# Loading token tiles in two groups ahead of the second weights, and regrouping the first products of a 2:4-pruned matrix product

## The chip, the cores and the metric

The kernel runs on one core of one Trainium2 chip. The metric is the device time in microseconds (us) of one execution, the median of several runs.

## What is computed

The weights `w` (1024 x 1024, bf16) are pruned 2 of 4: of each four neighbouring rows of a column, those two stay whose magnitude is the largest. The tokens `x` (16 x 512 = 8192 tokens of 1024 values) are multiplied with the pruned weights, and a bias is added.

```python
B, S, D = 16, 512, 1024
G = D // 4
wg = w.reshape(G, 4, D)
mag = jnp.abs(wg)
order = jnp.argsort(mag, 1)
thr = jnp.take_along_axis(mag, order[:, 2:3, :], 1)   # the second largest of four
mask = (mag >= thr).astype(w.dtype)
wp = (wg * mask).reshape(D, D)
return jnp.einsum("bsd,df->bsf", x, wp) + b
```

## The kernel before

The 8192 tokens are 64 tiles of 128. The 1024 rows of `w` are two groups g of 512; the columns of group 0 come in four pieces of 256 (pieces 0 to 3), those of group 1 in two of 512 (pieces 4 and 5). On the chip, the four members of a pruning group lie in one partition, as m = 0 to 3 of `w_sb`, so that VectorE can compare them: `abs` (magnitude), `hi` and `lo` (larger and smaller of two pairs), `t1`, `t2` and `thr` (the threshold), `mask`, and `mult` (the pruned weights, written to `wp`). These are the steps of the class `Piece` (from line 153).

There are two ways to multiply. In the natural way the pruned weights are moved by DMA from `wp` to `wp_nat` (`spread`, line 149), with the rows of `w` in the partitions, and the tokens come transposed by DMA (`xlead`, `xlow`, `xb`); this is `nat` (line 241), and nearly all of the work runs so. At the start, however, `wp_nat` isn't there yet. So the first seven tiles (0 to 6) are treated with group 0 in another way: they are loaded as they are (`load_x`, line 105), TensorE transposes each in four matmuls (`transpose`, line 194, token T), ScalarE copies the result from PSUM to SBUF (`copy_xt`, line 202, token C), and TensorE multiplies it straight with the pieces of `wp` as VectorE finishes them (`mm_piece`, line 215, token M; `M5.0t` is tile 5, piece 0, part t). A part is a choice of the members: u, v, s, t are m = 0, 1, 2, 3, x is the first two and y the last two. ScalarE copies finished sums of these products from PSUM to SBUF (`stage`, tokens S and U), where they wait for the other half of the product. Then follow the natural products: E and A open tiles 7 to 11, 24 half tiles are closed, and six batches of 8 tiles and one of 4 end the work.

The order on each engine is written out by hand. `order` (lines 267 to 289) holds one list of tokens for TensorE, VectorE, ScalarE and the SyncE queue; each engine executes its list in order. Ahead of the lists stand the loads, in the order of lines 122 to 134, split between the SyncE queue and, where "act" is given, ScalarE's queue:

```python
    load_w(0, 0, 256, 0, 2)
    load_w(0, 0, 256, 2, 4, "act")
    load_x(5, 6, "act")
    load_x(SOLO, SOLO + 1, "act")        # tile 6
    ...
    load_x(3, 5)
    load_w(0, 256, 512)                  # the second weights
    load_x(2, 3)
    load_x(0, 2)
```

The transposes write to a pool of two PSUM banks (`psum_t`); tile 4 alone takes one of the six banks of `psum_o`, where the products' sums lie too. A transpose therefore waits for the copy of the transpose two before it, except T4a. Before the lists TensorE runs 20 filler matmuls on constants, and the token F4 runs four more after T6a.

In SyncE's list W0.0 and W0.1 are the spreads of group 0's two column halves, W1.0p and W1.1 those of group 1 (W1.0q is on ScalarE's queue), Z the last weights and the bias, X1, Y1 and Y0 transposed loads.

Of the kernel before, what the change touches and what calls it, by code (L numbers as in the profile page):

```python
# [10 lines left out]
def kernel(  # L11
# [8 lines left out]
    P = 128  # L20
    bf16 = mybir.dt.bfloat16
    fp32 = mybir.dt.float32
# [10 lines left out]
    FH = 512  # L33
# [26 lines left out]
    psum_t = ctx.enter_context(tc.tile_pool(name="psum_t", bufs=2, space=bass.MemoryType.PSUM))  # L60
    psum_o = ctx.enter_context(tc.tile_pool(name="psum_o", bufs=6, space=bass.MemoryType.PSUM))
# [10 lines left out]
    def pe(i):  # L72
        return seq("pe", i)
# [4 lines left out]
    def act(i):  # L78
        return seq("act", i)

    def sp(i):
        return seq("sp", i)
# [10 lines left out]
    def tokens(dram, t):  # L93
        a, b_ = next(s for s in GROUPS if s[0] <= t < s[1])
        return dram[a * P:b_ * P].rearrange("(p t) k -> p t k", p=P), t - a
    bias_sb = const.tile([P, Dout], bf16)

    def issue(eng, out_, in_):
        q = nc.sync if eng == "sp" else nc.scalar
        return seq(eng, q.dma_start(out_, in_))  # L100

    def load_w(g, c0, c1, ma=0, mb=4, eng="sp"):
        issue(eng, w_sb[:, g, ma:mb, c0:c1], wv[:, g, ma:mb, c0:c1])

    def load_x(ta, tb, eng="sp"):
        xs = const.tile([P, tb - ta, HK], bf16, name=f"x_{ta}")
        xv, n = tokens(xf, ta)
        issue(eng, xs[:], xv[:, n:n + tb - ta, :HK])
        for t in range(ta, tb):
            x_sb[t] = xs[:, t - ta, :]  # L110
# [10 lines left out]

    load_w(0, 0, 256, 0, 2)
    load_w(0, 0, 256, 2, 4, "act")
    load_x(5, 6, "act")
    load_x(SOLO, SOLO + 1, "act")
    act(nc.scalar.activation(spark[:], nc.const_aps.tensor(1.0, [P, 1], bf16), Act.Abs))
    load_x(3, 5)
    load_w(0, 256, 512)
    load_x(2, 3)
    load_x(0, 2)  # L130
    load_w(0, 512, 768)
    load_w(0, 768, 1024)
    load_w(1, 0, 512)
# [7 lines left out]
    def filler(n, rep=1):  # L141
        for _ in range(n):
            pe(nc.tensor.matmul(warm_ps[:, :rep * P], lhsT=nc.const_aps.tensor(1.0, [P, P], bf16),  # L143
                                rhs=nc.const_aps.tensor(1.0, [P, rep * P], bf16), start=True, stop=True))
# [45 lines left out]
                self.tt(wp[:, self.g, ms, self.c0:self.c1], self.w[:, ms, :], self.mag[:, ms, :], Alu.mult)  # L190

    xpk = {}

    def transpose(t):
        xg = x_sb[t].rearrange("p (q m) -> p m q", m=4)
        bank = psum_o.tile([P, FH], fp32, name="ps") if t == 4 else psum_t.tile([P, FH], fp32, name="tp")
        tp = bank[:].bitcast(bf16)[:, :FH].rearrange("p (m q) -> p m q", m=4)
        for m in range(4):
            pe(nc.tensor.transpose(tp[:, m, :], xg[:, m, :], ident[:]))  # L199
        xpk[t] = tp  # L200
# [59 lines left out]
    def stage(key):  # L260
        solo = key[1] == "h"
        q, h, at = (pair_of[key[0]], key[2], int(key[0] != SOLO)) if solo else (key[0], key[1] // 2, key[1] % 2)
        if (q, h) not in staged:
# [2 lines left out]

    order = {
# [7 lines left out]
        ),  # L275
        "dve": (
# [4 lines left out]
        ),  # L281
        "act": (
            "C5a C3a C4a C6a C2a C0a C1a S3b0 S2b0 abs3 S0b0 U6h0 S3b1 S0b1 S2b1 S3b2 S0b2 S2b2 S2b3 S0b3 U6h1 "
            "S3b3 U7h0 W1.0q U7h1"
        ),
        "sp": (
            "W0.0 Z W0.1 X1 W1.0p Y1 Y0 W1.1"
# [1 line left out]
    }  # L289
    written = {"X0"}  # L290
    p = {}
    halves = {0: tuple("uvst"), 1: ('x', 'y'), 2: ('u', 'v', 'y'), 3: ('x', 'y')}

    by_rows = {0}

    def all_of(tok, i):
        return [tok + x for x in halves.get(i, ("",))]

    def split_tok(tok):
        k = tok[-1] if tok[-1] in "xyabuvst" else ""  # L300
        return (tok[:-1] if k else tok), k

    transposed = []

    def needs(eng, tok):
        base, k = split_tok(tok)
        if tok[0] == "C":
            return ["T" + tok[1:]]
        if tok[0] == "T":
            return ["C" + transposed[-2]] if tok != "T4a" and len(transposed) > 1 else []  # L310
        if tok[0] == "F":
            return []
        if tok[0] == "W":
            g, h = map(int, tok[1:4].split("."))
            return [n for i, pc in enumerate(pieces) if pc[0] == g and pc[1] // FH == h for n in all_of(f"mult{i}", i)]
        if tok[0] in "XYZ":
            return []
        if tok[0] == "A":
            return ["X0", f"W0.{tok.split('h')[1]}"] + ([f"U{NPK}h{tok[-1]}"] if tok[1] == "3" else [])
        if tok[0] == "E":  # L320
            return ["X0", f"W0.{tok[1]}"]
        if tok[0] == "U":
            t, h = map(int, tok[1:].split("h"))
            if t == NPK:
                return [f"E{h}"]
            return [f"M{t}.{x}" for i, pc in enumerate(pieces) if pc[0] == 0 and pc[1] // FH == h for x in all_of(str(i), i)]
        if base[0] == "M":
            t, i = base[1:].split(".")
            return [f"C{t}a", f"mult{i}{k}"]
        if tok[0] == "S":  # L330
            q, n = map(int, tok[1:].split("b"))
            return [f"M{t}.{x}" for i, pc in enumerate(pieces) if pc[0] == 0 and pc[1] // CW == n
                    for t in pairs[q] for x in all_of(str(i), i)]
        i, step = base[-1], base[:-1]
        before = {"abs": [], "hi": ["abs"], "lo": ["abs"], "t1": ["hi"], "t2": ["lo"],
                  "thr": ["t1", "t2"], "mask": ["thr", "hi", "lo"], "mult": ["mask"]}[step]
        out_ = []
        for b_ in before:
            if b_ in ("abs", "hi", "lo") and int(i) in by_rows:
                out_ += [b_ + i + k] if step in ("hi", "lo") else [b_ + i + s for s in "ab"]  # L340
            else:
                out_.append(b_ + i + (k if b_ == "mask" else ""))
        return out_

    def emit(eng, tok):
        base, k = split_tok(tok)
        if tok[0] == "T":
            transpose(int(tok[1:-1]))
            if tok != "T4a":
                transposed.append(tok[1:])  # L350
        elif tok[0] == "F":
            filler(int(tok[1:]))
        elif tok[0] == "W":
            g, h = map(int, tok[1:4].split("."))
            spread(g, h * FH, (h + 1) * FH, {"": range(4), "p": range(2), "q": range(2, 4)}[tok[4:]], eng)
        elif tok[0] == "Z":
            load_w(1, 512, 1024)
            sp(nc.sync.dma_start(bias_sb[:], b.partition_broadcast(P)))
        elif tok[0] == "X":
            xnat.update(load_lead(int(tok[1:])))  # L360
        elif tok[0] == "Y":
            xnat.update(load_low(int(tok[1:])))
        elif tok[0] == "E":
            open_solo(int(tok[1:]))
        elif tok[0] == "U":
            t, h = map(int, tok[1:].split("h"))
            stage((t, "h", h))
        elif tok[0] == "A":
            open_nat(*map(int, tok[1:].split("h")))
        elif tok[0] == "C":  # L370
            copy_xt(int(tok[1:-1]))
        elif tok[0] == "M":
            mm_piece(*map(int, base[1:].split(".")), part[k])
        elif tok[0] == "S":
            stage(tuple(map(int, tok[1:].split("b"))))
        else:
            i = int(base[-1])
            if i not in p:
                p[i] = Piece(i)
            if eng == "act":  # L380
                p[i].abs_act()
            else:
                p[i].do(base[:-1], part[k], half.get(k, slice(0, 2)))
# [82 lines left out]
    for bi, (tb, nb) in enumerate(batches):  # L466
        if bi:
            load_batch(bi + 1)
        for j in range(nb):
            t = tb + j  # L470
            xt = xnat[t]
            o = outp.tile([P, Dout], bf16, name="o")
            if t == NT - 1:
                for n, (c0, c1) in enumerate(((0, FH), (FH, FH + CW), (FH + CW, Dout - P), (Dout - P, Dout))):
                    ps = psum_o.tile([P, FH], fp32, name="ps")
# [44 lines left out]
```

## Time and profile before

| | |
|---|---|
| time, median of 3 runs | 233.68 us (233.33 to 234.12) |
| span of the profiled execution, first to last instruction | 232.0 us |
| time beside the span, median less span | 1.7 us |
| TensorE busy | 226.2 us, 98% of the span |
| VectorE busy | 107.9 us, 47% |
| ScalarE busy | 13.3 us, 6% |
| DMA read and written in HBM | 3.28 MB and 16.78 MB |
| group 0's direct products (line 229) | 112 matmuls of 256 columns |
| natural products (line 243), the three largest groups | 831, 63 and 47 matmuls of 512 columns |

The profile is of one execution. Only the span is shown in it, and no time of its own for the execution around the span; the second but one row above takes the median of the runs. A matmul's listed duration contains its passage through the array, so durations of neighbours overlap; the spacing of their starts is the better measure. "idle before" in a row is the time in which that engine did nothing, with what ended it.

### The profile page before, as it was taken

What the parts mean: (1) busy time and instruction counts of PE and PEld (TensorE: products, weight loads), DVE (VectorE), ACT (ScalarE), POOL (GpSimd) and SP (SyncE); (2) the same over time, 40 slices, a digit from 0 to 9 for tenths busy, and PEclk for the clock granted to TensorE, in tenths of its full rate; (3) what the DMA queues carried; (4) which work ended last, traced back from release to release, by engine and by line L of the source; (5) the groups of instructions that cost most, each with busy time, mean ns of one, the idle gap of its engine ahead of it and who ended that gap; (6) DMA issues with size and microseconds to landing.
All of it is one profiled execution on the core that took longest, in us unless ns stands there. A gap on an engine that the chain in (4) does not pass through costs nothing.

```text
span 232.0 us, 2815 instructions
## 1 busy us (share of the span) xinstructions
PE 226.2 (98%) x1128; PEld 110.4 (48%) x1148; DVE 107.9 (47%) x194; ACT 13.3 (6%) x26; POOL 17.6 (8%) x15
## 2 busy tenths in 40 slices
PE   7899999999999999999999999999999999999995
PEld 4786444444444444444444444444444444444443
DVE  4899967754234334334324324424424423423434
ACT  2576100000000000000000000000000000000000
POOL 1000099800000000000000000000000000000000
PEclk9999999999999999999999999999999999999999
DMA  6999999997299321991239721797229952122122
GB/s 201 255 193 266 261 182 230 277 312 271 95 206 259 123 93 54 261 273 45 93 103 275 210 90 51 146 240 212 81 90 184 241 163 77 61 90 90 48 90 90
DMA packets 79292, 38.19 MB, mean 165 GB/s; under 512 B 64176, under 2 KB 71728, under 8 KB 79280
## 3 DMA queue, kind: packets, MB, share of 16 engines
q1 hardware_dynamic: 68352, 20.75, 43.5%
q10 hardware_dynamic: 10928, 17.27, 21.1%
q8 instruction: 9, 0.15, 0.3%
q14 instruction: 3, 0.02, 0.0%
HBM read 3.28 MB, written 16.78 MB: 86 GB/s over the span
## 4 chain that ended last, share of the span: by engine, by line
PE 96%; DMA 2%; issue 1%; ACTq 0%; DVE 0%
PE ps L243 87%; PE ps L229 5%; PE tp L243 2%; DMA x<-in_x_dram 2%; PE tp L199 1%; ACTq L100 0%; DVE o L428 0%; PE ps L143 0%
## 5 line engine op out<-in xcount | busy, mean ns | idle before, releaser
L243 PE MATMUL ps<-wp_nat,xb 128*128 128x512 bf16 (+1 forms) x831 | 178.9, 375 | 0.9
L243 PEld LDWEIGHTS <-xb 128*128 128x128 bf16 x848 | 82.4, 98 | 97.5
L428 DVE TENSOR_TENSOR o<-ps,bias_sb 128x512 bf16<-128x512 f32 (+1 forms) x112 | 71.6, 677 | 113.8 <-PE ps L243 111.5
L424 POOL TENSOR_TENSOR st<-st,bias_sb 128x1024 f32<-128x1024 f32 x8 | 16.7, 2124 | 0.0
L243 PE MATMUL ps<-wp_nat,xlead 128*128 128x512 bf16 x63 | 14.7, 379 | 0.1
L243 PEld LDWEIGHTS <-xlead 128*128 128x128 bf16 x88 | 8.6, 98 | 10.2
L229 PE MATMUL ps<-wp,xt 128*128 128x256 bf16 x112 | 12.9, 273 | 0.0
L430 DVE TENSOR_TENSOR o<-ps,st 128x512 bf16<-128x512 f32 x16 | 11.1, 692 | 2.8 <-PE ps L243 2.2
L229 PEld LDWEIGHTS <-xt 128*128 128x128 bf16 x112 | 10.8, 98 | 1.2
L243 PE MATMUL ps<-wp_nat,xlow 128*128 128x512 bf16 x47 | 10.6, 379 | 0.1
L265 ACT COPY st<-ps 128x512 f32<-128x512 f32 x14 | 7.4, 594 | 3.0 <-PE ps L229 3.0
L243 PEld LDWEIGHTS <-xlow 128*128 128x128 bf16 x48 | 5.0, 103 | 5.4
L164 DVE TENSOR_TENSOR wp<-w_sb,mag 128x256 bf16<-128x256 bf16 (+2 forms) x13 | 6.2, 482 | 0.1
L164 DVE TENSOR_TENSOR mag<-mag,hi 128x256 bf16<-128x256 bf16 (+2 forms) x13 | 6.0, 482 | 0.2
L243 PE MATMUL tp<-wp_nat,xlead 128*128 128x512 bf16 x23 | 5.8, 379 | 0.0
L143 PE MATMUL ps<-const-bfloat16-1.0 128*128 128x128 bf16 (+1 forms) x24 | 4.1, 334 | 0.8 <-PEq L504 0.8
L174 DVE TENSOR_SCALAR mag<-w_sb 128x512 uint16<-128x512 uint16 (+2 forms) x6 | 2.7, 468 | 4.2 <-DMA w_sb<-in_w_dram 4.2
L199 PE MATMUL tp<-ident,x 128*128 128x128 bf16 x24 | 2.2, 224 | 1.3 <-DMA x<-in_x_dram 1.3
L143 PEld LDWEIGHTS <-const-bfloat16-1.0 128*128 128x128 bf16 x24 | 2.1, 118 | 2.4 <-issue 2.4
L164 DVE TENSOR_TENSOR hi<-mag 128x512 bf16<-128x512 bf16 (+2 forms) x7 | 3.2, 456 | 0.0
L164 DVE TENSOR_TENSOR lo<-mag 128x512 bf16<-128x512 bf16 (+2 forms) x7 | 3.1, 457 | 0.0
L199 PEld LDWEIGHTS <-x 128*128 128x128 bf16 x28 | 1.8, 115 | 2.0 <-DMA x<-in_x_dram 2.0
(18 smaller groups left out, 15.0 us busy)
## 6 DMA issues: line engine op xcount, KB each, us to landing
out_dram<-o ACTq DMA_DIRECT2D x58, 256.0 KB, 2.4
wp_nat<-wp SPq DMA_DIRECT2D x14, 128.0 KB, 3.3
out_dram<-o ACTq DMA_DIRECT2D x10, 128.0 KB, 1.7
w_sb<-in_w_dram SPq DMA_DIRECT2D x2, 512.0 KB, 5.3
w_sb<-in_w_dram SPq DMA_DIRECT2D x3, 256.0 KB, 5.9
x<-in_x_dram SPq DMA_DIRECT2D x2, 256.0 KB, 4.7
x<-in_x_dram ACTq DMA_DIRECT2D x2, 128.0 KB, 4.3
bias_sb<-in_b_dram SPq DMA_DIRECT2D x1, 256.0 KB, 4.7
```

The lines of the kernel that those rows point to most:

```text
L143: pe(nc.tensor.matmul(warm_ps[:, :rep * P], lhsT=nc.const_aps.tensor(1.0, [P, P], bf16), rhs=nc.const_aps.tensor(1.0, [P, rep * P], bf16), ...
L164: dve(nc.vector.tensor_tensor(out, a, b_, op=op))
L174: dve(nc.vector.tensor_single_scalar(self.mag[:, ms, :].bitcast(u16), self.w[:, ms, :].bitcast(u16), 0x7FFF, op=Alu.bitwise_and))
L199: pe(nc.tensor.transpose(tp[:, m, :], xg[:, m, :], ident[:]))
L229: pe(nc.tensor.matmul(ps[:, c0 + d:c1 + d], lhsT=xpk[t][:, m, :], rhs=wp[:, g, m, c0:c1], start=(new and m == ms.start), stop=(left[key] = ...
L243: pe(nc.tensor.matmul(ps, lhsT=xt[:, kt - koff, :], rhs=wp_nat[:, kt, c0:c1], start=(kt == first), stop=(kt == last)))
L265: act(nc.scalar.copy(staged[(q, h)][:, at, :, :].rearrange("p t c -> p (t c)"), ps_open.pop(key)[:]))
L424: pool(nc.gpsimd.tensor_tensor(st[:], st[:], bias.to_broadcast([P, 2, 2, CW]), op=Alu.add))
L428: dve(nc.vector.tensor_tensor(o[:, c0:c1], ps, bias_sb[:, c0:c1], op=Alu.add))
L430: dve(nc.vector.tensor_tensor(o[:, c0:c1].rearrange("p (n c) -> p n c", n=2), ps.rearrange("p (n c) -> p n c", n=2), add, op=Alu.add))
```

## The change

The loads of x are regrouped: tile 5 moves from ScalarE's queue into one load with tiles 3 and 4 on SyncE's, and tiles 0 to 2 become one load, issued ahead of the second weights. Tile 6 is then the only x load on ScalarE's queue. On TensorE tile 6 is transposed first, the token F4 is dropped, and the four products M6.0t, M5.0t, M3.0t, M4.0t stand ahead of the transposes of tiles 2, 0 and 1, which now follow one another; the other products go part by part over all seven tiles. Tile 1's transpose takes a bank of `psum_o`, as tile 4's does. On VectorE piece 0's `hi` and `lo` are one step each instead of two, its four parts become three (s, t and x), piece 1 has the parts s, t and x instead of x and y, and piece 2's `abs` moves to ScalarE, ahead of the copies S.

```diff
     load_w(0, 0, 256, 0, 2)
     load_w(0, 0, 256, 2, 4, "act")
-    load_x(5, 6, "act")
     load_x(SOLO, SOLO + 1, "act")
     act(nc.scalar.activation(spark[:], nc.const_aps.tensor(1.0, [P, 1], bf16), Act.Abs))
-    load_x(3, 5)
+    load_x(3, 6)
+    load_x(0, 3)
     load_w(0, 256, 512)
-    load_x(2, 3)
-    load_x(0, 2)
     load_w(0, 512, 768)
...
+    OWN = (4, 1)
 
     def transpose(t):
         xg = x_sb[t].rearrange("p (q m) -> p m q", m=4)
-        bank = psum_o.tile([P, FH], fp32, name="ps") if t == 4 else psum_t.tile([P, FH], fp32, name="tp")
+        bank = psum_o.tile([P, FH], fp32, name="ps") if t in OWN else psum_t.tile([P, FH], fp32, name="tp")
...
         "pe": (
-            "T5a T3a T4a T6a F4 M5.0t M3.0t M5.0s M3.0s M4.0t M4.0s T2a M6.0s M3.0u M6.0u M5.0u T0a M4.0u T1a "
-            "M2.0s M2.0t M2.0u M6.0t M0.0u M0.0s M0.0t M1.0t M0.0v M2.0v M1.0v M5.0v M6.0v M3.0v M4.0v M1.0u "
...
+            "T6a T5a T3a T4a M6.0t M5.0t M3.0t M4.0t T2a T0a T1a M2.0t M0.0t M1.0t M6.0s M5.0s M3.0s M4.0s M2.0s "
+            "M0.0s M1.0s M3.0x M4.0x M6.0x M5.0x M2.0x M0.0x M1.0x M3.1t M4.1t M6.1t M5.1t M2.1t M0.1t M1.1t "
...
         "dve": (
-            "abs0a abs0b hi0a lo0a lo0b hi0b t20 t10 thr0 mask0t mask0s mult0t mult0s mask0u abs1 mult0u hi1 lo1 "
-            "t11 t21 mask0v thr1 mult0v mask1y mask1x mult1y abs2 mult1x lo2 hi2 t22 t12 thr2 mask2y mask2v "
...
+            "abs0a abs0b lo0 hi0 t20 t10 thr0 mask0t mask0s mult0t mask0x mult0s mult0x abs1 hi1 lo1 t11 t21 thr1 "
+            "mask1t mask1s mult1t mask1x mult1s mult1x lo2 hi2 t22 t12 thr2 mask2y mask2v mult2y mask2u mult2v "
...
         "act": (
-            "C5a C3a C4a C6a C2a C0a C1a S3b0 S2b0 abs3 S0b0 U6h0 S3b1 S0b1 S2b1 S3b2 S0b2 S2b2 S2b3 S0b3 U6h1 "
-            "S3b3 U7h0 W1.0q U7h1"
+            "C6a C5a C3a C4a C2a C0a C1a abs2 S0b0 S3b0 S2b0 abs3 S0b1 U6h0 S3b1 S2b1 S0b2 S3b2 S2b2 S0b3 U6h1 "
+            "S3b3 S2b3 U7h0 W1.0q U7h1"
         ),
...
-    halves = {0: tuple("uvst"), 1: ('x', 'y'), 2: ('u', 'v', 'y'), 3: ('x', 'y')}
+    halves = {0: ('s', 't', 'x'), 1: ('s', 't', 'x'), 2: ('u', 'v', 'y'), 3: ('x', 'y')}
...
-            return ["C" + transposed[-2]] if tok != "T4a" and len(transposed) > 1 else []
+            return ["C" + transposed[-2]] if int(tok[1:-1]) not in OWN and len(transposed) > 1 else []
```

More of the change, by code (lines that the diff above doesn't have):

```diff
@@ L338, in needs @@
         for b_ in before:
-            if b_ in ("abs", "hi", "lo") and int(i) in by_rows:
-                out_ += [b_ + i + k] if step in ("hi", "lo") else [b_ + i + s for s in "ab"]
+            if b_ == "abs" and int(i) in by_rows:
+                out_ += [b_ + i + s for s in "ab"]
             else:
@@ L348, in emit @@
             transpose(int(tok[1:-1]))
-            if tok != "T4a":
+            if int(tok[1:-1]) not in OWN:
                 transposed.append(tok[1:])
```

12 rows, old and new, of the table order are left out of this document.

## The prediction, made before the changed kernel had run

> **What bounds the kernel now.** I read first the page's busy times and slices, then TensorE's timeline of the first 36 us, then the timelines of ScalarE, VectorE and the load queues, and last the DMA issues in narrow windows, which give each load's time to landing.
>
> ```profile
> span 232.0 us, 2815 instructions
> PE 226.2 (98%) x1128; PEld 110.4 (48%) x1148; DVE 107.9 (47%) x194; ACT 13.3 (6%) x26; POOL 17.6 (8%) x15
> PEclk9999999999999999999999999999999999999999
> ...
> 0.77 3.66 PE L143 MATMUL ps<-const-bfloat16-1.0 128*128 128x512 bf16 x20 [0.77 <-PEq L504]
> 5.10 0.64 PE L199 MATMUL tp<-ident,x 128*128 128x128 bf16 x8 [0.67 <-DMA x<-in_x_dram]
> 5.57 0.39 PE L199 MATMUL ps<-ident,x 128*128 128x128 bf16 x4
> 6.60 0.41 PE L199 MATMUL tp<-ident,x 128*128 128x128 bf16 x4 [0.64 <-DMA x<-in_x_dram]
> 6.85 0.39 PE L143 MATMUL ps<-const-bfloat16-1.0 128*128 128x128 bf16 x4
> 7.08 0.82 PE L229 MATMUL ps<-wp,xt 128*128 128x256 bf16 x6
> 7.81 0.41 PE L199 MATMUL tp<-ident,x 128*128 128x128 bf16 x4
> 8.96 0.39 PE L199 MATMUL tp<-ident,x 128*128 128x128 bf16 x4
> 9.18 11.19 PE L229 MATMUL ps<-wp,xt 128*128 128x256 bf16 x101
> 20.20 1.03 PE L243 MATMUL tp<-wp_nat,xlead 128*128 128x512 bf16 x4
> ```
>
> The columns of a timeline are start, length, then what ran, with the idle time before it in brackets. TensorE is busy 98% of the span and shows no idle time from 7.08 on, so the end follows when TensorE gets through its opening. That is: fillers, the transposes T of seven tiles, and the 112 products M of line 229, ending at 20.20 where E0 (line 243) begins. The last 101 products take 20.20 - 9.18 = 11.02 us, 0.109 us each. From 7.08 to 20.20 there are 13.12 us; 112 products are 12.22 us, three transposes (T2a, T0a, T1a, 0.23 us each by the step from 5.10 to 5.57 for two) are 0.69 us, so only 0.21 us of this stretch is waiting. The change leaves the number of products and transposes as it is and everything after E0 too. What it can win or lose is the start of the products and waits among them. It cannot win more than it finds there.
>
> **The loads.** These rows are issues of the load queues and then, from windows around each issue, the time to landing:
>
> ```profile
> 1.26 0.98 ACTq L100 DMA_DIRECT2D x<-in_x_dram  x2
> ...
> 1.24 0.46 SPq L100 DMA_DIRECT2D x<-in_x_dram  x1
> 1.74 0.67 SPq L100 DMA_DIRECT2D w_sb<-in_w_dram  x1
> 2.46 1.08 SPq L100 DMA_DIRECT2D x<-in_x_dram  x2
> ...
> x<-in_x_dram SPq DMA_DIRECT2D x1, 256.0 KB, 4.0
> x<-in_x_dram ACTq DMA_DIRECT2D x1, 128.0 KB, 3.8
> w_sb<-in_w_dram SPq DMA_DIRECT2D x1, 256.0 KB, 5.7
> x<-in_x_dram ACTq DMA_DIRECT2D x1, 128.0 KB, 4.8
> x<-in_x_dram SPq DMA_DIRECT2D x1, 128.0 KB, 5.3
> x<-in_x_dram SPq DMA_DIRECT2D x1, 256.0 KB, 5.4
> ```
>
> Issue plus time to landing gives: tile 5 at 1.26 + 3.8 = 5.06, tiles 3-4 at 1.24 + 4.0 = 5.24, tile 6 (issued some 0.5 later than tile 5) at 1.78 + 4.8 = 6.58, the second weights at 1.74 + 5.7 = 7.44, tile 2 at 2.46 + 5.3 = 7.76, tiles 0-1 at about 3.1 + 5.4 = 8.5. With the first weights (two halves of 128 KB) ahead of all, the bytes landed are 640 KB by 5.24, 768 KB by 6.58, 1024 KB by 7.44, 1152 KB by 7.76 and 1408 KB by 8.5. This table is how I move loads: a load lands when the bytes queued up to and with it have landed before.
>
> After the change, tile 6 stands second on ScalarE's queue, where tile 5 stood: 5.06. Tiles 3-5 end the first 768 KB, so the nearest row is tile 6's 6.58; the other end is 5.24 plus 128 KB at the rate of the weights after it (256 KB from 6.58 to 7.44, so 0.43), 5.67. I take 6.4, near the upper end, because the same bytes landed then, and a little earlier because no weights run beside the last third now. Tiles 0-2 end 1152 KB: 7.76. The second weights end 1408 KB: 8.5 instead of 7.44. The third weights keep the bytes ahead of them.
>
> The Trainium skill ("DMA: Bandwidth & Descriptors", Queues, rings and completion order) says that a DMA engine takes turns between the queues that have work. By that rule tile 6, alone on its queue, passes the first third of tiles 3-5; the trace agrees as far as tiles 5 and 3-4 landed 0.2 us apart.
>
> **The opening, step by step.** ScalarE's copies C turn a transposed tile into an operand:
>
> ```profile
> 5.55 0.65 ACT L204 COPY xt<-tp 128x256 f32<-128x256 f32 x2 [1.79 <-PE tp L199]
> 6.08 0.39 ACT L204 COPY xt<-ps 128x256 f32<-128x256 f32 x1
> 8.27 0.37 ACT L204 COPY xt<-tp 128x256 f32<-128x256 f32 x1 [0.85 <-PE tp L199]
> 9.05 0.70 ACT L204 COPY xt<-tp 128x256 f32<-128x256 f32 x2 [0.41 <-PE tp L199]
> 11.72 1.06 ACT L167 ACTIVATE mag<-w_sb 128x1024 bf16<-128x1024 bf16 x1
> ```
>
> A copy starts 0.45 us after its transposes began (5.10 to 5.55, 7.81 to 8.27), takes 0.37, and the next follows 0.27 later (5.55, some 5.82, 6.08). Before, TensorE has something between a transpose and the product that needs it: while tile 6 is awaited the copies of 5, 3 and 4 finish, then 6 products cover T2a's start, 4 products its copy, and 101 products follow T1a, most of them of other tiles.
>
> After: T6a at 5.10, and its copy is long done. T5a, T3a, T4a start at a = 6.45 and end at a + 0.70. M6.0t goes at a + 0.70. M5.0t needs C5a, ready at a + 0.82, and starts with its weight load at about a + 0.90; M3.0t needs C3a, a + 1.09, start a + 1.18; M4.0t needs C4a, a + 1.37, start a + 1.45, over at a + 1.55. Three transposes and four products would fill only 1.14, so 0.41 us is waiting, where before it was free. T2a starts at s = a + 1.55 = 8.0, behind tiles 0-2 (7.76), so that landing is just covered. T2a, T0a, T1a end at s + 0.70. M2.0t waits for C2a to s + 0.93, M0.0t for C0a to s + 1.23, M1.0t for C1a to s + 1.53, over at s + 1.64; 0.61 us is waiting. The other 21 products of piece 0 are at hand on TensorE only now, since it runs in order and M6.0s stands behind M1.0t in the list.
>
> Sum: the products begin at 6.45 + 0.70 = 7.15 instead of 7.08 (+0.07; the four fillers F4, 0.23 us before 7.08, go, and tile 6 is no longer last, but tiles 3-5 are, with three transposes behind). Then 12.22 + 0.69 + 0.41 + 0.61 = 13.93 us instead of 13.12 (+0.81). E0 starts at 21.08 instead of 20.20: +0.88, taken as +0.9 us.
>
> **What must not become late.** VectorE's rows:
>
> ```profile
> 5.80 0.49 DVE L164 TENSOR_TENSOR wp<-w_sb,mag 128x256 bf16<-128x256 bf16 x2
> 7.43 0.43 DVE L174 TENSOR_SCALAR mag<-w_sb 128x1024 uint16<-128x1024 uint16 x1 [0.94 <-DMA w_sb<-in_w_dram]
> 7.97 0.42 DVE L164 TENSOR_TENSOR hi<-mag 128x512 bf16<-128x512 bf16 x1
> 8.31 0.42 DVE L164 TENSOR_TENSOR lo<-mag 128x512 bf16<-128x512 bf16 x1
> 8.64 0.29 DVE L164 TENSOR_TENSOR hi<-hi 128x256 bf16<-128x256 bf16 x1
> 8.85 0.28 DVE L164 TENSOR_TENSOR lo<-lo 128x256 bf16<-128x256 bf16 x1
> 16.98 0.42 DVE L164 TENSOR_TENSOR wp<-w_sb,mag 128x512 bf16<-128x512 bf16 x1
> ```
>
> Steps follow at 0.34 us for 512 columns and 0.2 for 256, with about 0.1 more where a step needs the one just before. Piece 0's first product of VectorE comes at 5.8 + 0.28 as before: one larger step each for hi and lo replaces two smaller ones. The larger steps save some tenths on VectorE, and TensorE waits for none of them. Piece 1 starts at 8.5 and has its first part (abs, hi, lo, two, thr, two masks, mult) at 11.2; TensorE asks for it at s + 1.64 + 21 x 0.109 = 11.9. Piece 2: abs2 leaves VectorE for ScalarE at 1.06 us (the row of abs3), after the third weights at some 9.5, done at 10.6; mult2y then comes at about 14.4 and is wanted at 15.0. Piece 3's last mult is over at 18.0 instead of 17.40, wanted at 19.6. Cover of 0.6 to 1.6 us, so I cost these at nothing; with cover gone each 0.1 us late is 0.1 on the end. On ScalarE abs2 stands ahead of S0b0, S3b0, S2b0, abs3: these end at about 13.8 by 0.55 us a copy, and hi3 wants abs3 at 14.7; the PSUM banks that they free are wanted from 14.9.
>
> Behind, on SyncE, the spreads of the pruned weights wait for piece 1 and 3:
>
> ```profile
> 11.96 3.42 SPq L100 DMA_DIRECT2D wp_nat<-wp  x4
> 17.43 2.79 SPq L100 DMA_DIRECT2D wp_nat<-wp  x4
> wp_nat<-wp SPq DMA_DIRECT2D x14, 128.0 KB, 3.3
> ```
>
> The first four's last issue begins by 14.8 and lands by 18.1 against E0's 20.20; the second four's by 22.9, against E1 at some 24.5. VectorE's lateness of 0.6 us moves them by as much, TensorE moves by 0.9, so these covers of 1.6 to 2.1 us hold, and the rest of the span moves as a block. The profiled execution's span is 231.99; the median of the three runs is 233.68, 1.69 us more, which lies around the span and which I leave as it is. 233.68 + 0.9 gives 234.6.
>
> **Rivals.** *The tiles come early; no slower.* If tiles 3-5 land at 5.67, a is 5.72 and the first part is over at 7.27; T2a then waits only for tiles 0-2. By 1152 KB that is 7.8 and E0 20.9 (234.4); if they too come a microsecond early, s is 7.27 and E0 is 20.4 (+0.2, 233.9). With 5.24 for tiles 3-5 it is s = 6.85 and E0 19.95, 0.25 us faster, 233.4, and no row allows less. It decides from s = 7.1. For it: tile 6 landed 1.3 us after tiles 3-4 though only 128 KB lay between, so some of this is not bytes. Against: such a delay would be as likely in the new load. Chance 0.28.
>
> *VectorE becomes the bound.* If the second weights land at the third's place, 9.5 instead of 8.5, mult1t comes at 12.2 and piece 2's first at 15.4, against 11.9 and 15.0: 0.4 us more, 235.0. For it: two larger x loads pass them on SyncE; against: the bytes ahead are the same as those ahead of tiles 0-1. Chance 0.10.
>
> *The clock falls.* Here TensorE idles more between 4.43 and 8.0 and F4 is gone. Before it was busy half of such a stretch and kept its clock:
>
> ```profile
> 4.43:7.08 2.65, 1.35 (x22) 1.19 (x21) 1.99 (x9) 0.96 (x4) 0.00 (x0) 1.00 1.09 336
> ```
>
> (length, busy times of PE, PEld, DVE, ACT, POOL, then clock 1.00.) The opening fillers show the slow rate: 6 of 512 and 14 of 128 columns in 3.66 us are 0.75 ns a column against 0.43 for a product. A slow stretch as long as that costs 3.66 x (1 - 0.43/0.75) = 1.6 us: 236.2. Chance 0.05.
>
> The Trainium skill ("TensorE: Matmul & The Clock Gate", Why this matters for your kernels) asks for no idle gaps over about 3 us and says (Part 4) that transposes do not count as busy; this rule speaks against the change, but its gaps are under 1.2 us each, and no run here shows a fall of the clock after such gaps.
>
> **The numbers.** The forecast case keeps 0.57. A measurement of this kernel can tell about 0.3%, 0.7 us, from no change. Slower by more than that: 0.47 of the forecast's 0.57, and the VectorE and clock cases, 0.62. Faster: 0.03, of the early tiles when they and the scatter of the runs go one way. Within: 0.35. The range reaches from the early tiles (233.4 to 233.9) to VectorE's case with tiles 3-5 at 6.58 (235.2) and some scatter of the runs (233.33 to 234.12 before): 233.5 to 235.6. It leaves out the clock case and the earliest tiles.
>
> **What would show it.** Right: on TensorE's timeline T6a near 5.1, T5a near 6.4, short waits for ScalarE's copies ahead of single products around 7 to 9.7, then no wait, and E0 near 21.1. Wrong: E0 before 20.3; waits for VectorE after 10 us; a clock under 1 after 4.4 us; waits for wp_nat at E0 or E1.

## The result and the profile after

The changed kernel takes 236.51 us (median of 4 runs, 236.31 to 237.62); the kernel before, on the same chip, 233.50 (233.04 to 234.12). The ratio is 1.0145, 95% interval 1.0116 to 1.0175: slower by 3.0 us by the medians, where 0.9 was forecast, and outside the range (233.5 to 235.6).

The page of the changed kernel, then TensorE's timeline (start, length, what ran, idle before it):

```profile
span 234.8 us, 2804 instructions
PE 228.3 (97%) x1124; PEld 111.7 (48%) x1144; DVE 107.9 (46%) x191; ACT 14.2 (6%) x27; POOL 17.6 (7%) x15
PEclk9799999999999999999999999999999999999999
...
0.77 4.21 PE L141 MATMUL ps<-const-bfloat16-1.0 128*128 128x512 bf16 x20 [0.77 <-PEq L503]
4.78 0.53 PE L198 MATMUL tp<-ident,x 128*128 128x128 bf16 x4
7.14 0.64 PE L198 MATMUL tp<-ident,x 128*128 128x128 bf16 x8 [1.82 <-DMA x<-in_x_dram]
7.61 0.39 PE L198 MATMUL ps<-ident,x 128*128 128x128 bf16 x4
7.83 1.12 PE L228 MATMUL ps<-wp,xt 128*128 128x256 bf16 x4
8.76 1.06 PE L198 MATMUL tp<-ident,x 128*128 128x128 bf16 x8
9.61 0.63 PE L198 MATMUL ps<-ident,x 128*128 128x128 bf16 x4
10.04 12.98 PE L228 MATMUL ps<-wp,xt 128*128 128x256 bf16 x108
22.85 1.03 PE L242 MATMUL tp<-wp_nat,xlead 128*128 128x512 bf16 x4
```

E0 (line 242 here) starts at 22.85 instead of 20.20: 2.65 of the 2.8 us by which the span grew lie ahead of it. The page shows a 7 in the second slice of the granted clock, where it was 9 throughout. The loads, from windows around their issues (tile 6 at 1.26, tiles 3-5 at 1.24, tiles 0-2 at about 2.0, the second weights at 2.6), the last number being the time to landing:

```profile
x<-in_x_dram ACTq DMA_DIRECT2D x1, 128.0 KB, 2.6
x<-in_x_dram SPq DMA_DIRECT2D x1, 384.0 KB, 5.9
x<-in_x_dram SPq DMA_DIRECT2D x1, 384.0 KB, 6.2
w_sb<-in_w_dram SPq DMA_DIRECT2D x1, 256.0 KB, 6.5
```

Tile 6 landed at 3.86, earlier than forecast (5.06); tiles 3-5 at 7.1 (6.4), tiles 0-2 at 8.2 (7.76), the second weights at 9.1 (8.5). T5a therefore starts at 7.14 instead of 6.45. The view of windows (stretch, its length, then busy time of PE, PEld, DVE, ACT, POOL with the number of instructions, granted clock, DMA share, GB/s) puts the clock beside the waiting, first in the changed kernel, then in the kernel before:

```profile
5.07:8.48 3.41, 1.58 (x19) 1.00 (x16) 1.85 (x7) 1.27 (x4) 0.00 (x0) 1.00 0.98 279
8.48:11.90 3.42, 3.39 (x22) 2.44 (x22) 2.67 (x10) 2.10 (x5) 0.00 (x0) 0.50 1.22 287
```

```profile
3.64:7.05 3.41, 2.11 (x33) 1.77 (x32) 2.78 (x13) 1.05 (x5) 0.00 (x0) 1.00 1.04 323
```

In the changed kernel TensorE is busy for 1.58 of 3.41 us, and the next 3.41 us go at half the clock; the transposes of tiles 2, 0 and 1 and the first of the 108 products lie in them. In the kernel before it is busy for 2.11, and the clock stays. Three of the four runs of the changed kernel show a mean clock of 0.993, which is one such window. The slowest, 237.62, shows 0.999, and no profile of it is at hand, so what slowed that one is not shown.

### The profile page after: what moved, and what is told of

It is laid out like the page before. It is cut to its first block, busy times and chain, and to the rows that moved or that the text cites. A ratio compares the mean times of both kernels' runs of the same rounds, so it can differ in the third digit from the quotient of the medians.

```text
span 234.8 us, 2804 instructions
## 1 busy us (share of the span) xinstructions
PE 228.3 (97%) x1124; PEld 111.7 (48%) x1144; DVE 107.9 (46%) x191; ACT 14.2 (6%) x27; POOL 17.6 (7%) x15
## 4 chain that ended last, share of the span: by engine, by line
PE 95%; DMA 2%; issue 1%; SPq 0%; DVE 0%
PE ps L242 86%; PE ps L228 6%; DMA x<-in_x_dram 2%; PE tp L242 2%; PE tp L198 1%; PE ps L198 0%; SPq L100 0%; DVE o L427 0%
## 5 line engine op out<-in xcount | busy, mean ns | idle before, releaser
L228 PE MATMUL ps<-wp,xt 128*128 128x256 bf16 x112 | 14.1, 283 | 0.0
L242 PEld LDWEIGHTS <-xlead 128*128 128x128 bf16 x88 | 8.6, 98 | 10.2
L198 PEld LDWEIGHTS <-x 128*128 128x128 bf16 x28 | 2.5, 132 | 2.1 <-DMA x<-in_x_dram 2.0
L162 DVE TENSOR_TENSOR hi<-mag 128x512 bf16<-128x512 bf16 (+1 forms) x6 | 3.1, 510 | 0.1
L162 DVE TENSOR_TENSOR lo<-mag 128x512 bf16<-128x512 bf16 (+1 forms) x6 | 3.1, 509 | 0.1
```

Source lines behind the costliest of these rows:

```text
L162: dve(nc.vector.tensor_tensor(out, a, b_, op=op))
L228: pe(nc.tensor.matmul(ps[:, c0 + d:c1 + d], lhsT=xpk[t][:, m, :], rhs=wp[:, g, m, c0:c1], start=(new and m == ms.start), stop=(left[key] = ...
L242: pe(nc.tensor.matmul(ps, lhsT=xt[:, kt - koff, :], rhs=wp_nat[:, kt, c0:c1], start=(kt == first), stop=(kt == last)))
```

## The experiments

The theory after the result had three parts: late loads (0.7 us against the forecast), the bare chains of copies, in which TensorE has nothing to do until ScalarE has copied a tile (the forecast 0.9), and one window of half clock (1.0 us: from T2a to E0 it is 22.85 - 8.76 = 14.09 us instead of the 13.1 of the forecast).

### One part of the change at a time

`e1_loads`: the kernel before with the changed loads alone.

```diff
-    load_x(5, 6, "act")
     load_x(SOLO, SOLO + 1, "act")
...
-    load_x(3, 5)
+    load_x(3, 6)
+    load_x(0, 3)
     load_w(0, 256, 512)
-    load_x(2, 3)
-    load_x(0, 2)
```

> The kernel before with the loads of the change alone; all four lists of instructions stay. Theory of the loads (tiles 3-5 and 0-2 on one queue land late, at about 7.1 and 8.2 us as in the changed kernel, and the wait lowers the clock): T5a near 7.1, first products near 8.0 instead of 7.08, E0 near 21.2, and near 22.2 if a window of half clock follows: +1.0 to +2.0 us, 234.5 to 235.5. Rival, theory of the order (the chains of copies that stand bare are the main cost): the loads alone cost under 0.4 us, 233.5 to 233.9, at full clock.

`e2_order`: the reverse, the changed kernel with the five old loads of x in their old places.

> The changed kernel with the loads of the kernel before; the order on all engines stays as changed. Theory of the order: T6a stands first and waits for tile 6 at about 6.55, T5a, T3a, T4a follow, T2a near 8.4, then 13.1 us to E0 at about 21.5: +1.3 us, 234.8, at full clock. Theory of the loads: with the old loads most of the 3 us goes, 233.9 to 234.3. If a window of half clock follows here too, 1.0 us is added to either.

Measured: e1 236.21 (ratio 1.0118, 1.0090 to 1.0146), e2 235.93 over ten runs (1.0098, 1.0069 to 1.0127). Each half alone costs nearly as much as the whole change; the costs do not add. e1 took longer than either of its theories allowed. TensorE's timeline of e1, then two windows of e2:

```profile
6.17 1.04 PE L197 MATMUL tp<-ident,x 128*128 128x128 bf16 x8 [1.19 <-DMA x<-in_x_dram]
...
8.29 1.48 PE L227 MATMUL ps<-wp,xt 128*128 128x256 bf16 x6
9.57 0.63 PE L197 MATMUL tp<-ident,x 128*128 128x128 bf16 x4
...
22.12 1.03 PE L241 MATMUL tp<-wp_nat,xlead 128*128 128x512 bf16 x4
```

```profile
5.07:8.48 3.41, 1.10 (x17) 0.99 (x18) 2.72 (x11) 0.69 (x3) 0.00 (x0) 1.00 1.08 317
8.48:11.90 3.42, 3.39 (x25) 2.19 (x23) 2.96 (x11) 2.40 (x6) 0.00 (x0) 0.50 1.27 179
```

In e1 T5a starts at 6.17, not near 7.1 as expected: in this profile the load of tiles 3-5 takes 4.9 us to landing instead of 5.9. The first six products take 9.57 - 8.29 = 1.28 us, 0.21 each, twice the usual 0.109: the clock had not been released at all by then, which happened only at 10.2. So this one profile shows the late clock more than the late load. The window ahead of the products, at the slow rate, was this:

```profile
3.38:6.79 3.41, 2.22 (x21) 1.96 (x20) 3.02 (x14) 0.00 (x0) 0.00 (x0) 1.00 0.86 256
```

(The view counts the clock as 1.00 until its first release.) In e2 the clock fell for one window, as in the changed kernel. The runs of e2 divide by it: the three at 234.15, 234.17 and 234.51 had a mean granted clock of 0.999 to 1.000, and all five with 0.993 (one window at half of a span of 234 us) lie between 235.9 and 236.7. The other two, 235.3 and 236.0, show 1.000; a late release does not lower this mean, as e1's profiled run shows (1.000), and may be what slowed them. So without that window the order alone costs about 1.0 to 1.4 us over the 233.12 of the kernel before on that chip, somewhat more than the 0.9 of the forecast's chains. Part of it may not be the chains: this order wants tile 6 first, and the old loads brought it after tiles 3 to 5 (at 7.1 in e2's profile).

### The clock by itself

`e3_fill`: the changed kernel with fillers where TensorE waits for tiles 3-5 anyway.

```diff
-            "T6a T5a T3a T4a M6.0t M5.0t ...
+            "T6a F30 T5a T3a T4a M6.0t M5.0t ...
```

> The changed kernel with 30 filler matmuls of 128 columns (1.7 us) between T6a and T5a, where TensorE waits for tiles 3-5 in any case. Theory of the clock (the wait of about 2 us and the short stops behind it brought one window of 3.4 us at half clock, worth 1.0 us): the granted clock stays 1.0 after the warm-up, E0 near 21.8 instead of 22.85, 235.5. Rival (the fall comes from the stops among the products, or its cost is hidden): clock and time as in the changed kernel, 236.5.

Measured: 235.43, all four runs between 235.21 and 235.74 with a clock of 1.000 (ratio 1.0088, 1.0060 to 1.0116; the changed kernel 1.0145). Its timeline and the window of the fillers:

```profile
6.96 0.64 PE L198 MATMUL tp<-ident,x 128*128 128x128 bf16 x8 [0.51 <-DMA x<-in_x_dram]
...
8.52 0.61 PE L198 MATMUL tp<-ident,x 128*128 128x128 bf16 x8
...
21.50 1.03 PE L242 MATMUL tp<-wp_nat,xlead 128*128 128x512 bf16 x4
```

```profile
3.70:7.10 3.40, 2.89 (x49) 2.72 (x47) 3.30 (x13) 0.37 (x1) 0.00 (x0) 1.00 0.80 220
```

Work that computes nothing takes 1.1 us off the time. The fall of the clock is shown, and its price: T2a to E0 is 12.98 us instead of 14.09, so 1.1 us of the 1.35 by which E0 comes earlier (0.18 is T5a, whose tiles landed that much sooner). T5a to T2a is 1.56 us and T2a to E0 12.98, as the forecast had them (1.55 and 13.1).

Three kernels set fillers in the waits of the other combinations: `g1_base_fill` (the kernel before: F8 ahead of T5a, F6 between T4a and T6a), `g2_loads_fill` (e1 with F30 ahead of T5a), `g3_order_fill` (e2 with F20 ahead of T6a).

> The kernel before, with its waits for x filled: 8 filler matmuls ahead of T5a and 6 between T4a and T6a. Theory (at full clock the loads and the order cost about 1 us each and add; the clock takes the rest): the kernel before loses nothing to the clock in most executions, so 233.0 to 233.5, and the scatter upwards (to 234.4) shrinks. Rival (the fillers are in the way of the transposes): 234 or more.

> The loads of the change with the old lists, as before, and 30 fillers ahead of T5a, where TensorE waits for tiles 3-5. Theory of two costs and the clock: the late and cold clock goes, and the loads alone cost what T5a and the second group come later, about 1 us: 234.0 to 234.4 instead of 236.2. Rival (the loads themselves cost all of it): 235.5 or more.

> The order of the change with the old loads, and 20 fillers ahead of T6a. Theory of two costs and the clock: the two groups of executions of the same kernel without fillers (234.2 to 234.5 and 235.3 to 236.7) become one near 234.2, about 1 us over the kernel before: the bare chains of copies that were forecast at 0.9. Rival (its spread has another cause than the clock): two groups as before.

Measured: 233.51 (1.0022), 235.25 (1.0089), 235.04 (1.0080). In the first, the kernel before gained nothing from fillers and its scatter did not shrink (233.08 to 234.57), but it is no clean test: in its profile the fillers ran to 5.63, ahead of a T5a that started at 5.10 without them. The second: at full clock the loads alone still cost 2.1 us, twice what was expected, while both parts together cost 2.3 at full clock (e3, 235.43 against 233.12) and the order alone 1.0 to 1.4. TensorE in g2:

```profile
7.10 0.64 PE L197 MATMUL tp<-ident,x 128*128 128x128 bf16 x8 [0.22 <-DMA x<-in_x_dram]
...
8.43 0.81 PE L227 MATMUL ps<-wp,xt 128*128 128x256 bf16 x6
```

T5a starts at 7.10 and the first product at 8.43, since the old list has all four transposes and F4 ahead of it, where the changed list starts at 7.83. Late loads hurt the old order more than the changed one, which goes some way to explain why the two parts do not add. The third was a poor test: its fillers ran to 6.79 on a clock that was released late, while tile 6 had landed at 5.6, so they stood in the way; it settles nothing.

### Why the loads are late

`e6_twoq` (tile 5 behind tile 6 on ScalarE's queue, tiles 3-4 in a load on SyncE's, tiles 0-2 as changed) and `h4_swapq` (tiles 3-5 on ScalarE's queue, tile 6 ahead of tiles 0-2 on SyncE's) ask whether one queue is too little:

> The changed kernel with tile 5 in a load of its own behind tile 6 on ScalarE's queue, tiles 3-4 on SyncE's; the rest as changed. Theory of one queue (two queues side by side move more than one; one alone moved about 0.2 MB per us from 3.5 to 6.3 us): tiles 3-5 land by 5.6, tiles 0-2 near 7.5, E0 at 20.5 to 21.0: 233.8 to 234.4. Rival, theory of the shape (x loads of three rows a partition are slow by themselves): tiles 0-2 still land after 8, T2a near 8.3, E0 at 21.4 or later: 234.7 or more.

> The changed kernel with the queues exchanged: tiles 3-5 on ScalarE's queue, tile 6 ahead of tiles 0-2 on SyncE's, so that tiles 3-5 and 6, 0-2 go side by side on two queues. Theory of one queue (one queue alone is slower than two): the x bytes move at 0.29 MB per us, tiles 3-5 land by 6 and tiles 0-2 by 7.2. Rivals (shape; x without weights): tiles 3-5 and 0-2 still land at 7 to 8, no gain.

Measured: 235.81 (1.0109) and 236.82 (1.0141, two runs, interval 1.0075 to 1.0207). The time to landing of e6's tiles 0-2, then of h4's tiles 3-5 and 0-2 (issued at about 1.8, 1.26 and about 1.8):

```profile
x<-in_x_dram SPq DMA_DIRECT2D x1, 384.0 KB, 6.1
x<-in_x_dram ACTq DMA_DIRECT2D x1, 384.0 KB, 6.3
x<-in_x_dram SPq DMA_DIRECT2D x1, 384.0 KB, 6.1
```

So tiles 0-2 land at 7.9 in e6, tiles 3-5 at 7.6 and tiles 0-2 at 7.85 in h4: the loads of three tiles are late on either queue. The theory of one queue falls. It falls by the landings, not by the times, which hold a lost clock as well: e6's profile had its release only at 9.7, and both runs of h4 show 0.993. (Tile 5, a load of one behind tile 6, came at 6.6 in e6; the kernel before had its tile 6 in that place at 6.58, so this says nothing of the shape.)

`h1_singles`, `h2_twoone` and `h3_wbetween` keep the queue and change the pieces or what is between them.

```diff
h2:
-    load_x(3, 6)
-    load_x(0, 3)
+    load_x(3, 5)
+    load_x(5, 6)
+    load_x(0, 2)
+    load_x(2, 3)
     load_w(0, 256, 512)
```

> The changed kernel with six loads of one tile each (3, 4, 5, 0, 1, 2) in place of the two loads of three; same queue, same bytes, same place ahead of the second weights. Theory of the shape (a load of three tiles goes slowly, since its rows of 1 KB lie next to each other): tile 5 lands by 5.9 instead of 6.9 to 7.1, tile 2 by 7.2 instead of 8.0 to 8.2; T5a (which waits for tile 5) near 5.9, about 1 us off the time. Rival (x alone on the queues, with no weights beside or among it, goes slowly whatever its pieces): tile 5 lands near 7 and tile 2 near 8, time as in the changed kernel, 236.5.

> The changed kernel with its two loads of three tiles cut as in the kernel before (3-4, 5, 0-1, 2), but still all on SyncE's queue ahead of the second weights. Theory of the shape: the pieces that went fast in the kernel before go fast again, tile 5 by 5.9, tile 2 by 7.2. Rival (x without weights among it): tile 5 near 7, tile 2 near 8.

> The changed kernel with the second weights issued between its two x loads. Theory of the shape: tiles 3-5 land as late as before, near 7, and tiles 0-2 near 8.5 to 9. Rival (x without weights among it): the second load overlaps with weights and goes at full rate, the weights land near 7.8 instead of 9.1; tiles 3-5 land somewhat earlier than 7, as less of tiles 0-2 is beside them.

Measured: h2 233.89 (1.0022, 1.0009 to 1.0035), h1 234.66 (1.0060), h3 236.03 (1.0107, two runs, 1.0008 to 1.0206). The time to landing of h2's tile 5 and tile 2 (issued at about 1.8 and 2.7):

```profile
x<-in_x_dram SPq DMA_DIRECT2D x1, 128.0 KB, 4.3
x<-in_x_dram SPq DMA_DIRECT2D x1, 128.0 KB, 4.5
```

In h2 the same bytes on the same queue in the same place land at 6.1 (tile 5) and 7.24 (tile 2); in h1 tile 5 at 5.6 and tile 2 at 6.7, though the second weights, behind more issues, land at 8.7 and TensorE waits 0.21 us for VectorE. In h3 tiles 3-5 come at 7.15, as in the changed kernel. The shape of the load it is: most of the 3.0 us go when the two loads of three tiles are cut in two each, the window of half clock with them (no run of h2 shows 0.993).

`k1_tilemajor` asks what it is in the shape. In this kernel token 3p + t of a group belongs to partition p of tile t, so the three rows that one load brings to a partition are neighbours of 2 KB in memory. k1 gives a tile 128 neighbouring tokens instead; the load keeps its number and size of pieces.

```diff
-        return dram[a * P:b_ * P].rearrange("(p t) k -> p t k", p=P), t - a
+        return dram[a * P:b_ * P].rearrange("(t p) k -> p t k", p=P), t - a
...
-        xq = xlow[:].rearrange("p k (q t) -> p k q t", t=b_ - a)
-        return {a + t: xq[:, :, :, t] for t in range(b_ - a)}
+        return {a + t: xlow[:, :, t * P:(t + 1) * P] for t in range(b_ - a)}
```

> The changed kernel with the tokens of tiles 0 to 5 assigned the other way: a tile is 128 neighbouring tokens instead of every third, so that the three rows of a partition in one load lie 256 KB apart instead of 2 KB (loads, transposed loads of the second half and stores all follow it). Same bytes, same number of pieces of 1 KB. Theory of neighbouring rows: tiles 3-5 land by 6.0 instead of 7, T5a near 6, about 234 us. Rival (three pieces a partition in one load are slow wherever they lie): tiles 3-5 near 7, 236 us or more.

Measured: 233.85 (1.0028, 1.0016 to 1.0039; seven runs, 233.59 to 234.23). Its loads of three tiles (issued at 1.24 and about 1.8) and TensorE:

```profile
x<-in_x_dram SPq DMA_DIRECT2D x1, 384.0 KB, 3.8
x<-in_x_dram SPq DMA_DIRECT2D x1, 384.0 KB, 5.3
...
7.10 0.64 PE L198 MATMUL tp<-ident,x 128*128 128x128 bf16 x8
...
20.12 1.03 PE L241 MATMUL tp<-wp_nat,xlead 128*128 128x512 bf16 x4
```

Tiles 3-5 land at 5.0 instead of 7.1, tiles 0-2 at 7.1 instead of 8.2. The DMA view over 3.5 to 6.3 us, while x is under way, for the kernel before, the changed kernel, e1, h2 and k1 in turn; it counts all that moves, not the loads of x alone:

```profile
DMA packets 1203, 0.88 MB, mean 314 GB/s; under 512 B 84, under 2 KB 1203, under 8 KB 1203
```

```profile
DMA packets 519, 0.50 MB, mean 178 GB/s; under 512 B 17, under 2 KB 519, under 8 KB 519
```

```profile
DMA packets 717, 0.69 MB, mean 247 GB/s; under 512 B 25, under 2 KB 717, under 8 KB 717
```

```profile
DMA packets 1119, 0.89 MB, mean 319 GB/s; under 512 B 76, under 2 KB 1119, under 8 KB 1119
```

```profile
DMA packets 858, 0.77 MB, mean 275 GB/s; under 512 B 42, under 2 KB 858, under 8 KB 858
```

With the loads of three neighbouring rows a partition, this stretch moves 178 GB/s in the changed kernel; with the same bytes in loads of two and one it moves 319, with the rows apart 275. The 178 is the lowest of its kind: e1, g2 and e3 have the same loads and moved 247, 189 and 213, and k5, with the loads of k1, moved 255. The landings part more clearly. Tiles 3-5 as three neighbours landed at 6.1 (e1) to 7.6 (h4) in six profiles, with the rows apart at 5.0 to 5.4 in three (k1, k5, k6). That the assignment decides it is shown; what happens in the memory or the DMA engines is not. The kernel before doesn't suffer: `k3_before_tilemajor` gives it the same assignment.

> The kernel before with the tokens of tiles 0 to 5 assigned as 128 neighbouring tokens a tile. Theory of neighbouring rows: its loads of two tiles have no neighbouring rows either then; x lands a little earlier and the lag of one or a few engines shrinks: 232.6 to 233.1. Rival: no change, 233.1 to 233.3.

Measured: 233.59 (1.0011, 0.9991 to 1.0030): no change, so loads of two neighbours are not slow.

### The order on loads that are not late

`k2_oldorder_twoone`: the old lists on h2's loads.

> The kernel before with all its lists, and the loads in pieces of 2 + 1 tiles on SyncE's queue ahead of the second weights, tile 6 first on ScalarE's queue. The changed order on these loads took 233.9. Theory (the changed order costs 0.9 by its bare chains of copies): 233.0 to 233.3, as the kernel before. Rival (the order costs nothing beside the loads, or the old order suits these loads as badly): 233.8 or more.

Measured: 234.14 (1.0056, 1.0030 to 1.0082), not less than h2's 233.89. Two of its seven runs lie apart: 235.44, the profiled one, had the clock released only at 10.1, and 235.67 looks like it. The others lie at 233.8 to 234.3. On these loads the old order is no better than the changed one. The forecast's 0.9 us is thus what the changed order costs on the old loads, not a price of its own: on these loads the old order loses about as much. Why it does is not shown, since k2's own profile is of a run with a late clock. Its first products wait for all four transposes, and in g2 some of piece 0 waited 0.20 us for VectorE steps that stand behind `abs1` in its list.

`k5_covered` takes k1 and puts the part s of tiles 6, 5, 3, 4 ahead of T2a and their part x behind T1a, so that no chain of copies stands bare; `k6_covered_wfirst` adds the second weights between the two loads of x and two more tokens (M6.0x and M5.0x, four products) ahead of T2a.

> The changed kernel with tokens assigned as 128 neighbours a tile (its loads of three tiles then land by 5.0 and 7.1; it took 233.85, E0 at 20.12), and in TensorE's list four products of part s ahead of T2a and the eight of part x behind T1a, so that C2a, C0a, C1a have products beside them. Theory of the bare chains: the wait ahead of T2a (0.6 us) and the 0.6 us behind it go, until piece 1 sets the end: its first part comes 2.7 us after the second weights (7.9), 10.6, then 84 products, E0 at 19.8: 233.4. Rival (these waits were not on the path): 233.8.

> The same with the second weights issued between the loads of tiles 3-5 and 0-2, and two more products ahead of T2a. Theory: second weights by 6.3 instead of 7.9, piece 1's first part at 9.7, tiles 0-2 by 7.4 in time for T2a near 7.5, products from 6.1 without a wait over 0.1, E0 near 19.2: 232.8 to 233.0, under the kernel before (233.1 to 233.3). Rival (one engine's lag on the loads, or VectorE, gives it back): 233.2 to 233.5.

Measured: k5 234.11 (1.0037), no better than k1; k6 233.39 (1.0004, 0.9994 to 1.0015). TensorE in k5, then in k6:

```profile
8.58 2.35 PE L228 MATMUL ps<-wp,xt 128*128 128x256 bf16 x20
11.47 9.55 PE L228 MATMUL ps<-wp,xt 128*128 128x256 bf16 x84 [0.55 <-DVE wp L162]
20.86 1.03 PE L241 MATMUL tp<-wp_nat,xlead 128*128 128x512 bf16 x4
```

```profile
8.87 11.08 PE L228 MATMUL ps<-wp,xt 128*128 128x256 bf16 x100
19.78 1.03 PE L241 MATMUL tp<-wp_nat,xlead 128*128 128x512 bf16 x4
```

In k5 the wait only changes its name: the 20 products follow one another, and TensorE then waits 0.55 us for VectorE's piece 1, whose weights landed late. With those weights early (k6) the wait is gone, and the changed order with late tiles 0-2 equals the kernel before, no more.

### Versions that might have beaten both

`e9_best` and `k4_best2` leave the loads of the kernel before and start its products ahead of T6a, with VectorE's `mult0u` and `mask0v` (in e9 `mult0v` too) ahead of `abs1`.

> The kernel before with its old loads, the products of tiles 5, 3, 4 moved ahead of T6a, and VectorE's mask0v, mult0u, mult0v moved ahead of abs1, where VectorE waits 0.9 us. Theory (the start of the products is set by tile 6, while mult0t is done at 6.1): products start near 6.2 instead of 7.08, E0 0.5 to 0.9 us earlier: 232.3 to 232.7. Rival (VectorE's second piece ends 0.4 us ahead of TensorE only, so an earlier start becomes a wait for it): 233.0 to 233.3, no change.

> The kernel before with its loads, and TensorE's list so that products of tiles 5, 3, 4 start before T6a, and every copy has products of other tiles beside it; VectorE's mask0v, mult0u ahead of abs1. Theory (start of the products at 6.2 instead of about 6.6 in a usual execution, VectorE's second piece as the next bound): E0 0.2 to 0.4 us earlier, 232.8 to 233.0. Rival (VectorE's second piece is wanted earlier by as much and is not there): 233.1 to 233.4.

Measured: 233.42 (1.0014, 1.0003 to 1.0025) and 233.25 (1.0007, 0.9995 to 1.0018). No version was faster than the kernel before. In k4 the products start at 6.33 and E0 at 19.64 in the profiled execution; but the 7.08 and 20.20 of the profile that the forecast rests on were a late execution of the kernel before, as the next section says. An estimate from those figures: 232.0 - 20.20 = 211.8 us lie behind E0, so an execution with the median span of 231.3 given there has E0 at about 19.5, and k4 has nothing to win over it.

## Why the prediction was wrong

**The direction and the first mechanism were right.** The trace of the changed kernel shows the chains as forecast: T5a to T2a 1.62 us (forecast 1.55), no wait of TensorE for VectorE, E0 and all behind it moved as a block. Where the clock stayed up, T2a to E0 took 12.98 us (e3) and 13.0 (k1), forecast 13.1.

**The step that failed first is the table of the loads**: "a load lands when the bytes queued up to and with it have landed before". It took the rate of the bytes from loads of one and two tiles, and put a load of three in their place. With that load under way all loads together moved 178 GB/s, and tiles 3-5 came at 7.14, 0.7 later than taken and 0.6 beyond the upper end of what the forecast allowed (6.58). What showed that it is the shape are h2 and k1. The size of the lateness scatters: in e1's profile the same load landed at 6.1. The table was wrong for tile 6 too, which came 1.2 us early, to no use, as TensorE then waited for tiles 3-5.

**The second step is the rival "the clock falls"**, with a chance of 0.05. Its mechanism and sign were right and it decided a third of the result. It was set aside because the gaps were to stay under 1.2 us, by a forecast landing that was itself too early; the gap became 1.82. By the busy share of a window, 2.11 of 3.41 us kept the clock in the kernel before, 1.58 and 1.10 lost it. By the longest single gap in such a window, 0.83 us (h2) kept it and 1.82 lost it, so the runs do not tell which of the two counts. The price (1.6 us, from the fillers) was too high: 1.0 against the forecast's 13.1 us, since a part of that window was waiting anyway. The rule of the Trainium skill cited there ("TensorE: Matmul & The Clock Gate") warns of gaps over about 3 us; here a gap of 1.82 us and the short stops behind it were enough, and the measurement decides. Counted with the transposes as not busy, as the prediction quotes the same page, the stretch without fillers or products is 4.98 to 7.83, 2.85 us, in the changed kernel and 4.43 to 6.85, 2.42 us, in the kernel before: so read, the rule is not far off, and the forecast's own stretch, 4.43 to 7.15 or 2.72 us, lay close to it.

**The sum**, put right with these two: 20.20 + 0.88 (as forecast) + 0.69 (T5a) + 0.07 (T5a to T2a) + 1.0 (clock) = 22.84; measured 22.85. The terms are read from the same two timelines and add up by themselves; the causes behind them rest on h2 and k1 (the loads) and on e3 (the clock). With 234.6 forecast this is 236.4, against 236.51.

**The base was late as well.** The profiled execution of before had a span of 232.0; 13 other executions, on another chip, ran from 230.9 to 232.6 with a median of 231.3. Tile 6, at 6.58 in that profile, landed at 5.4 to 5.6 in three other profiles with the same loads (g1, g3, k4), at 6.3 in e9 and at 7.1 in e2: a load can lag by over a microsecond without any change. The rival "the tiles come early" named such a lag, and the forecast compared a new load with a late old one.

**VectorE**, held back as a rival at 0.10, did not decide in the changed kernel; it becomes the bound as soon as the chains are covered (k5).

## What to carry to other kernels

Before a load is merged, look at which rows of memory it brings side by side; a term taken from smaller loads need not hold for the larger one, and a small variant (2 + 1 instead of 3) tells it in one run. Where TensorE waits in an opening, look at the longest gap and at the busy share over the clock's whole window, with and without the transposes, and hold them against windows that kept the clock. Two halves of a change that were made for each other can each cost as much as the whole; the test is both orders on both sets of loads.

## What had not been expected of the hardware

The granted clock changes in steps of 3.41 us whose phase differs from execution to execution: in the changed kernel it was released at 5.07 and halved from 8.48 to 11.90, in the kernel before released at 3.64, in e1 at 10.2. The same 20 fillers therefore took 3.66 us in one execution and 4.21 in another. In the profiles here a window with TensorE busy for 2.11 us or more of 3.41 kept the released clock, one with 1.58 or less lost it. To be released it took more: windows with 2.22 us (e1) and 2.62 us (k2) busy at the slow rate did not release it, so that 4.2 us of fillers across a bad phase were not enough, while one with 2.87 us did (the kernel before, 0.22 to 3.64). And a load of 384 KB with three neighbouring 1 KB pieces a partition took 4.9 to 6.3 us to landing in six profiles, against 3.8 to 4.2 in three for the same load with the pieces 256 KB apart.
